# Moving row stores, weight casts, token pieces, two weight sums and one subtraction in a hand-ordered attention and two-MoE kernel

## The chip, the cores and the metric

The kernel runs as one program on one core of a Trainium2 chip. The metric is the device time of one execution in microseconds (us); before the change it is 2083.56 us, the median of three runs (2080.17 to 2083.95). A core has five engines with a queue each, worked off in order: TensorE (PE, with its weight loads as PEld), VectorE (DVE), ScalarE (ACT), GpSimd (POOL) and SyncE (SP, which here only issues DMAs). They meet at semaphores.

## The reference, cut to what matters

Linear attention with a positive feature map feeds a dense mixture of experts (all 8 experts for all tokens, weighted by a Sinkhorn-normalised gate), and its output feeds a second mixture in which each token goes to one expert.

```python
# attention: 4 x 8 heads, 576 tokens, head_dim 64, 128 features; x becomes 2304 tokens x 512
q_p, k_p = phi(q), phi(k)                  # phi: x @ w_phi minus its max |.|, exp(+) and exp(-)
attn = (q_p @ (k_p.T @ v)) / (q_p @ sum(k_p) + 1e-6)
# first MoE: E = 8 experts, D = 512, F = 1024
P = sinkhorn(exp(x @ w_gate - max))        # 8 rounds over rows and columns
x = sum(P[:, e] * (relu(x @ w1[e]) @ w2[e]) for e in range(8))
# second MoE: one expert for each token
logits = norm(x) @ norm(expert_emb).T / tau
idx, gate_w = argmax(logits, 1), softmax(logits).max(1)
out[mask_e] = gate_w * (relu(x[mask_e] @ w1[e]) @ w2[e])
```

## The kernel before

**Numbers.** Every fp32 operand of a large matmul is split into a high part (an fp32r copy, made by ACT) and a rest (source minus high part, made by DVE or POOL). A product is three matmuls for each pair: high by high, high by rest, rest by high.

**Stages.** Attention runs first (to about 222 us of the span). The first MoE then runs in 48 half-steps `h`: 16 groups `n` (an expert's half), each over three blocks of 768 tokens. Both layers of a group are written as Strassen-Winograd products: seven products of quarter matrices in place of eight. Groups 0, 1 and 15 ("plain", `p1_group` and `p2_plain`) use them for the first layer alone; groups 2 to 14 ("mixed", `layers`) for both layers, with 14 products of twelve matmuls in a half-step. The names are those of the algorithm: A11, S1, S2, ... are weight quarters and their sums, B11, T1, T2, ... token or hidden quarters and their differences; `hb["T1"]` is the hidden T1, `xs["T1"]` the tokens' T1. Then comes routing (logits, argmax, counting, an indirect scatter of token numbers into `ids`, and storing the token rows to `x2d` in DRAM), and the second MoE (`second`) runs over 22 blocks of 128 gathered rows, each with one expert's weights.

**Order.** Nothing is reordered by a scheduler: the instructions stand on each queue as the code emits them. A half-step is a generator that yields after each product; after each yield, the loop runs what a table (`sched`) holds for that half-step and tick (`run_at`). The numbers in the tables of `ops_at`, `route_steps` and `tail` are ticks: they set where an operation stands in the queues among the products. In `tail`, ticks from 40 on are in the last half-step, where ticks 40 to 53 follow its 14 first-layer products and 54 to 69 its 16 second-layer products.

**In `layers`** (lines 479 to 571) the hidden quarters are made on the way. After the product A22 the code adds `u2c` to its bank `b2`, makes T1's rest from bank `b0` (DVE), gates `b2` in place (DVE, line 442), copies B21's high part (ACT, line 471), and then subtracts `b0` from `r22` to get T2 (DVE, line 486) and copies T2's high part. The fourth product of the second layer, S1 by T1, goes to a new tile `Z = pair(qz)`, which takes the bank of `b0`; so it can begin only when every reader of `b0` is done.

**Weight preparation.** For mixed groups the weights of the next group are summed (`S1r`, `S3r`, `S2r`, `S4r`, POOL, line 351) and split (ACT line 345, POOL line 346) during the third half-step of a group, at ticks of `ops_at(h, ...)`. In the same half-step POOL also makes the rests of the hidden quarters (line 474).

**Token pieces.** In half-steps 0 and 1 the next block's token quarters are loaded ("load"), subtracted on DVE (T3a, T1a, T2a, T4a, line 390) and split (ACT line 382, DVE line 383), at ticks of the same kind.

**The end of the first MoE.** `route_steps(6, ...)` routes tokens 768 to 1535 in the last two half-steps: `route_s` and `route_w` (DVE) make the gate weight, and `route_w` then stores six pieces of 128 rows of 513 numbers with SP (line 954); the last two pieces lie in `raw` tiles. `load_regs` has SP read the block table, `load_raws` has SP load the first expert's eight weight pieces of 512 KB (line 1074). `start_second` opens a pool (`m2r`) over the region in which the token tiles and the `raw` tiles lay. `first_w1(0, (c,))` casts weight piece `c` into that pool (ACT line 1102), makes its rest (DVE line 1103), and has SP load the next block's piece if its expert differs. `load_ids` has SP read the scattered token numbers (line 1058), six small loads a block, and `gather` has POOL fetch the rows. SP's DMAs go round eight semaphores; a DMA waits until the one eight places ahead of it on SP's queue has landed.

Of the kernel before, what the change touches and what calls it, by code (L numbers as in the profile page):

```python
# [32 lines left out]
RB = 6  # L33
# [12 lines left out]
def build(tc, a, out):  # L46
# [14 lines left out]
    V, A, G, T, SP = nc.vector, nc.scalar, nc.gpsimd, nc.tensor, nc.sync  # L61
# [28 lines left out]
    ids = [dr.tile([NSLOT, 1], I32, name=f"ids{k}") for k in range(RB)]  # L90
# [347 lines left out]
    def gate(out, th, src):  # L438
        g_ = hb["gate"][:, th * TH:(th + 1) * TH]
        if len(src.shape) == 3:  # L440
            g_ = g_.unsqueeze(1).to_broadcast([P, 2, TH])
        V.scalar_tensor_tensor(out=out, in0=src, scalar=0.0, in1=g_, op0=ALU.max, op1=ALU.mult)
# [27 lines left out]
    def high(nm, src):  # L470
        A.copy(hb[nm][:, 0], src)  # L471

    def rest(nm, src, eng):
        eng.tensor_tensor(out=hb[nm][:, 1], in0=src, in1=f32(hb[nm][:, 0]), op=ALU.subtract)  # L474
# [6 lines left out]
    def layers(h, n, bi):  # L481
        odd = h % 2
        qx, qz = (0, 3) if odd else (3, 0)

        def tt(out, x, y, op=ALU.subtract):
            V.tensor_tensor(out=out, in0=x, in1=y, op=op)  # L486

        def read(q_, ps, op=ALU.add):
            z = acc(bi)[:, q_]
            V.tensor_tensor(out=z, in0=z, in1=ps, op=op)  # L490

        b0 = pair(qz)
        yield from twin(b0, 1, "A11", xs["B11"], True)
        m1c = hraw("a")
        A.copy(m1c, b0)  # L495
        yield
        for nm in ("B11", "T1", "B21", "B22"):
            hb[nm] = hp.tile([P, 2, 2, TH], F32R, tag="h" + nm, name=f"h{nm}")
        for nm in ("T2", "T3", "T4"):
            hb[nm] = live["h3"].tile([P, 2, 2, TH], F32R, tag="h" + nm, name=f"h{nm}")  # L500
        hx = dict(hb)
        hb["gate"] = gates.popleft()

        yield from twin(b0, 1, "S2", xs["T2"], False)
        u2c = hp.tile([P, 2, TH], F32, tag="tu", name="u2c")
        A.copy(u2c, b0)
        b1 = pair(1)
        yield from twin(b1, 1, "A12", xs["B21"], True)
        tt(b1, b1, m1c, ALU.add)
        r11 = hraw("b")  # L510
        gate(r11, 0, b1)
        high("B11", r11)
        yield from twin(b0, 1, "S1", xs["T1"], False)
        rest("B11", r11, G)
        vc = hraw("c")
        A.copy(vc, b0)
        b2 = pair(2)
        yield from twin(b2, 1, "S3", xs["T3"], True)
        tt(b1, b2, vc, ALU.add)
        r22 = hraw("d")  # L520
        gate(r22, 1, b1)
        high("B22", r22)
        for i, _ in enumerate(twin(b0, 1, "S4", xs["B22"], False)):
            if i == 0:
                rest("B22", r22, G)
            yield
        gate(b0, 1, b0)
        t3 = hraw("c")
        tt(t3, r22, b0)
        high("T3", t3)  # L530
        tt(b0, b0, r11)
        high("T1", b0)
        for i, _ in enumerate(twin(b2, 1, "A22", xs["T4"], False)):
            if i == 0:
                rest("T3", t3, G)
            yield
        tt(b2, b2, u2c, ALU.add)
        rest("T1", b0, V)
        gate(b2, 0, b2)
        high("B21", b2)  # L540
        tt(r22, r22, b0)
        high("T2", r22)
        X = pair(qx)
        for i, _ in enumerate(twin(X, 2, "A11", hx["B11"], True)):
            if i == 0:
                rest("T2", r22, G)
            yield
        Y = pair(1)
        yield from twin(Y, 2, "S4", hx["B22"], True)
        read(1, Y, ALU.subtract)  # L550
        read(0, X)
        rest("B21", b2, V)
        Z = pair(qz)
        yield from twin(Z, 2, "S1", hx["T1"], True)
        t4 = hraw("a")
        tt(t4, r22, b2)
        high("T4", t4)
        read(1, Z)
        for i, _ in enumerate(twin(Y, 2, "S3", hx["T3"], False)):
            if i == 0:  # L560
                rest("T4", t4, G)
            yield
        read(3, Y)
        yield from twin(X, 2, "S2", hx["T2"], False)
        read(1, X)
        W_ = pair(2)
        yield from twin(W_, 2, "A12", hx["B21"], True)
        read(0, W_)
        yield
        w22 = wt[2, "A22"]  # L570
        yield from twin(Z, 2, w22, hx["T4"], False)
        read(2, Z, ALU.subtract)
        yield
# [381 lines left out]

    def route_i(t0, i):
        si = rt[t0]["si"]
        G.indirect_dma_start(out=ids[i % RB], out_offset=bass.IndirectOffsetOnAxis(si[:, i:i + 1], 0), in_=tokid[:, t0 + i:t0 + i + 1], in_offset=None)

    meta = c0.tile([1, 3, NBLK], I32, name="meta")  # L960
    ebx = c0.tile([1, NBLK + 1], F32, name="ebx")
# [230 lines left out]
    def first_w1(i, cs):  # L1192
        for c in cs:
            wsplit(i, 1, c)
            wcond(i + 1, 1, c)
# [10 lines left out]
    def ops_at(h, table, ops):  # L1206
        for i, names in table:
            for nm in names.split():
                at_tick(h + i // 40, i % 40, ops[nm])
# [19 lines left out]
    for h, (n, bi) in enumerate(HS):  # L1229
        nxt = HS[h + 1][1] if h + 1 < NH else bi  # L1230
        if nxt != bi:
            if n:
                for nm in XMIX if mixed(n) else XUSE:
                    at_tick(h, XFREE[nm][mixed(n)], partial(xreload, nxt, XUSE.index(nm)))
            else:
                ops = x_tasks(nxt, scratch(h), V)
                if h == 0:
                    ops_at(h, ((filled[0], "load"), (18, "B11"), (19, "T3a T1a"), (20, "T2a T2"), (21, "T3"), (22, "T1"), (23, "B21 T4a"), (24, "T4"), (25, "B22")), ops)
                else:
                    ops_at(h, ((1, "load"), (3, "T3a"), (5, "T1a"), (7, "T2a"), (14, "T2"), (15, "T1"), (16, "B11"), (17, "T3"), (18, "B21"), (19, "T4a"), (20, "T4"), (21, "B22")), ops)  # L1240
        if h % NB == NB - 1 and n + 1 < NGR:
            o1, o2 = wops(1, n + 1), wops(2, n + 1, SL1 if n == 0 else SL15 if n == NGR - 2 else {})
            if mixed(n):
                ops_at(h, ((2, "A11"), (3, "S1r"), (4, "S3r"), (5, "S2r"), (8, "A12"), (9, "S4r"), (10, "S2"), (12, "S1"), (14, "S3"), (16, "S4"), (18, "A22 load")), o1)
            else:
                ops_at(h, ((8, "A11"), (9, "S1r"), (10, "S3r"), (11, "S2r"), (13, "A12"), (14, "S4r"), (16, "S2"), (18, "S1"), (20, "S3"), (22, "S4"), (24, "A22 load")), o1)
            if n == 0:
                ops_at(h, ((24, "A11"), (25, "A12"), (26, "A21"), (28, "A22 load")), o2)
            elif n == 1:
                ops_at(h, ((22, "S1r"), (23, "S3r"), (24, "A12"), (26, "A22"), (28, "S3"), (40, "A11"), (41, "S2r"), (42, "S4r"), (44, "S1"), (46, "S4"), (49, "S2 load")), o2)  # L1250
            elif n == NGR - 2:
                ops_at(h, ((18, "A11"), (24, "A21"), (28, "A12"), (40, "A22 load")), o2)
            else:
                ops_at(h, ((18, "A11"), (20, "S1r"), (21, "S3r"), (25, "S2r"), (40, "A12"), (41, "S4r"), (43, "S1"), (45, "A22"), (46, "S4"), (49, "S3"), (51, "S2 load")), o2)
        if h >= 2 * NB - 1 and h + 1 < NH:
            at_tick(h, 20, partial(load_gate, HS[h + 1][0] // 2, nxt))
        if n == NGR - 1:
            for k, (i, j, op) in enumerate(FROM_Z):
                at_tick(h, 2 + 2 * k, partial(z_op, bi, i, j, op, G))
# [25 lines left out]
    rf = first_blocks()  # L1285

    tail = route_steps(0, (2, 4, 6, 8, 10, 12), (1, 2, 3, 4, 5, 6), p=13, b=14, o=16, s=18, c=19, d=21, w=23, i=(23, 23, 24, 25, 26, 27))
    tail += route_steps(6, (26, 28, 40, 43, 45, 47), (25, 26, 27, 42, 43, 44), p=48, b=46, o=47, c=49, d=49, i=(50, 50, 50, 51, 53, 54), s=54, w=56)
    tail += [(k, partial(next, rf, None)) for k in (50, 51, 52, 53, 55)] + [(54, partial(load_regs, i)) for i in range(2)]
    tail += [(54, partial(load_raws, 1, range(4))), (54, partial(load_raws, 2, range(4))), (56, early_second), (56, start_second)]  # L1290
    tail += [(62 + 2 * c, partial(first_w1, 0, (c,))) for c in range(4)]
    tail += [(63 if i < 2 else 67, partial(load_ids, i)) for i in range(NEARLY)]
    tail += [(67, partial(gather, 0)), (68, partial(gather, 1))]
    for i in range(3):
# [53 lines left out]
    def second(i0, i1):  # L1348
# [15 lines left out]
        i = i0  # L1364
        if i0 == 0:
            t0 = NA
            for k in range(3, NTL - NA):
                route_l(t0, k)
                route_a(t0, k)
# [146 lines left out]
```

## Time and profile before

| | us |
|---|---|
| median of three runs | 2083.56 |
| the profiled execution | 2082.38 |
| its span | 2080.5 |
| TensorE busy in the span | 1978.9 (95%) |
| DVE, POOL, ACT busy | 1296.1 (62%), 1057.5 (51%), 868.2 (42%) |
| TensorE's granted clock, mean | 0.985 |

TensorE is the bound: it is busy 95% of the span, and the page's 40 slices show 9 tenths in nearly all of them. The exceptions are the first slice (8) and the seven slices from 32 on that read 9, 3, 8, 8, 9, 9, 9: slice 33 alone has 3 tenths, and there the clock row falls to 7 and 8. So the questions to such a profile are where TensorE sits idle, and who ends each wait. In the timeline a row is start, duration, engine, line, operation, out<-in, shapes, count, and in brackets the idle time before it and what ended it. In a table of stretches a row is the stretch, its length, then the busy time and the number of instructions of PE, PEld, DVE, ACT and POOL, the granted clock, the share of time of the DMA engines, and GB/s. In a table of waits a row is who waited for whom, the sum, the number of times, and the longest.

### The profile page before, as it was taken

To read this page: it belongs to the slowest core of one execution; us is meant where nothing else is said; L and a number is where in the kernel's file an instruction comes from. 1 tells how busy PE (TensorE), PEld (TensorE's weight loads), DVE (VectorE), ACT (ScalarE), POOL (GpSimd) and SP (SyncE) were. 2 spreads that over 40 slices of the span, in tenths; PEclk is the share of its full clock that TensorE was granted. 3 is DMA by queue.
4 is the path that set the end of the run, shared out by engine and by line. 5 is a ranking of instruction groups with operands and counts; after the bars stand their busy time and mean duration, and the time that the engine had idled before them with its cause. 6 is when DMAs were issued, how large, how long until landed. Compare 5 with 4: busy or idle time off the path is not lost. (4 is left out here: it accounts for less than half of the span.)

```text
span 2080.5 us, 31444 instructions
## 1 busy us (share of the span) xinstructions
PE 1978.9 (95%) x11627; PEld 1886.8 (91%) x11627; DVE 1296.1 (62%) x1838; ACT 868.2 (42%) x1391; POOL 1057.5 (51%) x811
## 2 busy tenths in 40 slices
PE   8999999999999999999999999999999993889998
PEld 8999989999999999999999999999999993778886
DVE  6766556466656655655665565565566452589996
ACT  5566432223332433333242333334233231668785
POOL 1256102566574846657484665748375431345543
PEclk9999999999999999999999999999999997899999
DMA  3345633553625435373543537263453366334861
GB/s 119 113 141 182 223 138 147 138 193 101 247 86 194 154 122 188 107 249 81 204 143 133 177 110 246 80 216 124 152 174 110 114 145 112 51 99 151 289 232 63
DMA packets 138287, 314.63 MB, mean 151 GB/s; under 512 B 30456, under 2 KB 85256, under 8 KB 138130
## 3 DMA queue, kind: packets, MB, share of 16 engines
q1 hardware_dynamic: 134034, 302.06, 44.8%
q0 software_dynamic: 4096, 10.51, 1.8%
q8 instruction: 94, 1.54, 0.3%
q14 instruction: 63, 0.52, 0.1%
HBM read 335.81 MB, written 32.28 MB: 177 GB/s over the span
## 5 line engine op out<-in xcount | busy, mean ns | idle before, releaser
L490 DVE TENSOR_TENSOR acca<-acca,Q 128x768 f32<-128x768 f32 x182 | 170.5, 952 | 157.8 <-PE Q L428 157.8
L346 POOL TENSOR_TENSOR w1A<-raw,w1A 128x512 fp32r<-128x512 f32 x48 | 62.0, 1291 | 212.7 <-ACT w1A L345 132.8
L426 PE MATMUL Q<-hT,w2S 128*128 128x384 f32 x468 | 159.5, 341 | 9.8 <-ACT hB L471 9.8
L474 POOL TENSOR_TENSOR hB<-rb,hB 128x768 fp32r<-128x768 f32 x39 | 71.9, 1844 | 179.7 <-PE Q L428 179.7
L426 PE MATMUL Q<-xT,w1S 128*128 128x384 f32 x468 | 156.4, 334 | 0.9 <-ACT ra L495 0.9
L427 PE MATMUL Q<-hT,w2S 128*128 128x384 f32 x468 | 156.6, 335 | 0.0
L428 PE MATMUL Q<-hT,w2S 128*128 128x384 f32 x468 | 156.5, 334 | 0.0
L428 PE MATMUL Q<-xT,w1S 128*128 128x384 f32 x468 | 156.4, 334 | 0.0
L427 PE MATMUL Q<-xT,w1S 128*128 128x384 f32 x468 | 156.3, 334 | 0.0
L490 DVE TENSOR_TENSOR accb<-accb,Q 128x768 f32<-128x768 f32 x91 | 85.0, 952 | 84.3 <-PE Q L428 84.3
L1103 DVE TENSOR_TENSOR s1l<-rw,s1h 128x1024 fp32r<-128x1024 f32 x88 | 106.2, 1251 | 47.1 <-ACT s1h L1102 47.1
L495 ACT COPY ra<-Q 128x768 f32<-128x768 f32 x39 | 31.3, 802 | 207.9 <-PE Q L428 172.8
L486 DVE TENSOR_TENSOR Q<-Q,ra 128x768 f32<-128x768 f32 x39 | 37.7, 966 | 124.6 <-PE Q L428 124.6
L1102 ACT CAST s1h<-rw 128x1024 fp32r<-128x1024 f32 x88 | 88.5, 1062 | 60.1 <-DMA x2d<-raw 37.5
L474 POOL TENSOR_TENSOR hT<-rd,hT 128x768 fp32r<-128x768 f32 x39 | 72.3, 1853 | 66.0 <-ACT hT L471 66.0
L426 PEld LDWEIGHTS Q<-hT,w2S 128*128 128x128 f32 x468 | 87.8, 188 | 19.8 <-ACT hB L471 19.8
L426 PE MATMUL Q<-xB,w1A 128*128 128x384 f32 x312 | 104.3, 334 | 0.7 <-DVE accb L843 0.7
L428 PE MATMUL Q<-xB,w1A 128*128 128x384 f32 x312 | 104.2, 334 | 0.0
L427 PE MATMUL Q<-xB,w1A 128*128 128x384 f32 x312 | 104.2, 334 | 0.0
L426 PE MATMUL Q<-hB,w2A 128*128 128x384 f32 x312 | 104.2, 334 | 0.0
L427 PE MATMUL Q<-hB,w2A 128*128 128x384 f32 x312 | 104.2, 334 | 0.0
L428 PE MATMUL Q<-hB,w2A 128*128 128x384 f32 x312 | 104.2, 334 | 0.0
(428 smaller groups left out, 6663.7 us busy)
## 6 DMA issues: line engine op xcount, KB each, us to landing
xT<-xpd SPq DMA_DIRECT2D x120, 768.0 KB
rw<-in_moe_w SPq DMA_DIRECT2D x176, 512.0 KB
xB<-xpd SPq DMA_DIRECT2D x90, 768.0 KB
raw<-in_moe_w SPq DMA_DIRECT2D x34, 512.0 KB
gate<-gd SPq DMA_DIRECT2D x45, 384.0 KB
rx<-in_moe_w SPq DMA_DIRECT2D x30, 512.0 KB
xpd<-xT SPq DMA_DIRECT2D x12, 768.0 KB
xpd<-xB SPq DMA_DIRECT2D x9, 768.0 KB
```

What stands on the lines that cost most here:

```text
L346: eng.tensor_tensor(out=t[:, 1], in0=r(nm), in1=f32(t[:, 0]), op=ALU.subtract)
L426: T.matmul(bank, w[:, 0, j, k, :], x[:, 0, k, :], start=start and k == 0, stop=False, skip_group_check=True)
L427: T.matmul(bank, w[:, 0, j, k, :], x[:, 1, k, :], start=False, stop=False, skip_group_check=True)
L428: T.matmul(bank, w[:, 1, j, k, :], x[:, 0, k, :], start=False, stop=stop and k == 1, skip_group_check=True)
L474: eng.tensor_tensor(out=hb[nm][:, 1], in0=src, in1=f32(hb[nm][:, 0]), op=ALU.subtract)
L486: V.tensor_tensor(out=out, in0=x, in1=y, op=op)
L490: V.tensor_tensor(out=z, in0=z, in1=ps, op=op)
L495: A.copy(m1c, b0)
L1102: A.copy(hi, r)
L1103: V.tensor_tensor(out=lo, in0=r, in1=f32(hi), op=ALU.subtract)
```

## The change

It moves things and neither adds nor removes an instruction on the computing engines (`ids[i % RB]` becomes `ids[i]`, which is the same tile for the values of `i` that occur).

- In `layers`, the subtraction for T2 and the copy of its high part stand ahead of B21's gate and copy.
- In mixed groups, the sums `S1r` and `S3r` for the next group's first layer are made at ticks 4 and 8 of the second half-step, not at ticks 3 and 4 of the third.
- In half-steps 0 and 1 the token pieces stand at other ticks, one at a time and two ticks apart towards the end; in half-step 1 the first subtractions move from ticks 3, 5 and 7 to 14 and 15.
- At the end of the first MoE, `route_s` moves from tick 54 to 50 and `route_w` with its stores from 56 to 52; the steps of the block table (`rf`) and the weight loads move one tick later. The casts of the first block's weights move from ticks 62, 64, 66, 68 to 65, 67, 69 and, for the fourth, into `second`. The loads of token numbers for blocks 0 and 1 stay at tick 63.

```diff
@@ layers
         rest("T1", b0, V)
+        tt(r22, r22, b0)
+        high("T2", r22)
         gate(b2, 0, b2)
         high("B21", b2)
-        tt(r22, r22, b0)
-        high("T2", r22)
@@ token pieces, half-step 1
-                    ops_at(h, ((1, "load"), (3, "T3a"), (5, "T1a"), (7, "T2a"), (14, "T2"), (15, "T1"), (16, "B11"), (17, "T3"), (18, "B21"), (19, "T4a"), (20, "T4"), (21, "B22")), ops)
+                    ops_at(h, ((2, "load"), (14, "T3a T1a"), (15, "T2a B11"), (16, "T2"), (18, "T3"), (20, "T1"), (22, "B21 T4a"), (24, "T4"), (26, "B22")), ops)
@@ weight sums of mixed groups
-                ops_at(h, ((2, "A11"), (3, "S1r"), (4, "S3r"), (5, "S2r"), (8, "A12"), ...
+                ops_at(h - 1, ((4, "S1r"), (8, "S3r")), o1)
+                ops_at(h, ((2, "A11"), (5, "S2r"), (8, "A12"), ...
@@ routing and the first weights
-    tail += route_steps(6, ..., p=48, b=46, o=47, c=49, d=49, i=(50, 50, 50, 51, 53, 54), s=54, w=56)
-    tail += [(k, partial(next, rf, None)) for k in (50, 51, 52, 53, 55)] + [(54, partial(load_regs, i)) for i in range(2)]
-    tail += [(54, partial(load_raws, 1, range(4))), (54, partial(load_raws, 2, range(4))), (56, early_second), (56, start_second)]
-    tail += [(62 + 2 * c, partial(first_w1, 0, (c,))) for c in range(4)]
+    tail += route_steps(6, ..., p=47, b=46, o=47, c=49, d=49, i=(50, 50, 50, 51, 53, 54), s=50, w=52)
+    tail += [(k, partial(next, rf, None)) for k in (51, 52, 53, 54, 56)] + [(55, partial(load_regs, i)) for i in range(2)]
+    tail += [(55, partial(load_raws, 1, range(4))), (55, partial(load_raws, 2, range(4))), (56, early_second), (56, start_second)]
+    tail += [(65 + 2 * c, partial(first_w1, 0, (c,))) for c in range(3)]
@@ second, i0 == 0
             t0 = NA
+            first_w1(0, (3,))
```

DVE in a mixed half-step, as a difference (`Q_341` is the bank `b2`, `Q_339` the bank `b0`, `rd` is `r22`):

```order
 L486 TENSOR_TENSOR Q_341_5110<-Q_341_5110,u2c 128x2x384
 L474 TENSOR_TENSOR hT_5038<-Q_339_5012,hT_5038 128x768
+L486 TENSOR_TENSOR rd<-rd,Q_339_5012 128x768
 L442 SCALAR_TENSOR_TENSOR Q_341_5110<-Q_341_5110,gate_2_4919 128x2x384
-L486 TENSOR_TENSOR rd<-rd,Q_339_5012 128x768
 L490 TENSOR_TENSOR accb<-accb,Q_343_5185 128x768
```

The last DVE instruction that reads `b0` now stands one place sooner, and the gate of `b2` one place later; the rest of DVE's order is as it was.

SP at the end of the first MoE, before (`rows6a` to `raw` are the six pieces of token rows, `rw` the weight pieces):

```order
L1074 ISA
L1074 DMA rw_3_15982<-in_moe_w 128x1024
L954 DMA x2d<-rows6a 128x513
L954 DMA x2d<-rows6b 128x513
L954 DMA x2d<-rows6c 128x513
L954 DMA x2d<-rows6d 128x513
L954 DMA x2d<-raw_15602 128x513
L954 DMA x2d<-raw_15603 128x513
L1074 ISA
L1074 DMA rw_0_15968<-in_moe_w 128x1024
```

and in the changed kernel, at the place where the stores now stand:

```order
L954 DMA x2d<-rows_2_15264 128x2x513
L954 DMA x2d<-rows6a 128x513
L954 DMA x2d<-rows6b 128x513
L954 DMA x2d<-rows6c 128x513
L954 DMA x2d<-rows6d 128x513
L954 DMA x2d<-raw_15602 128x513
L954 DMA x2d<-raw_15603 128x513
L1045 TENSOR_LOAD meta
```

The six stores were behind all eight weight loads; now they follow the first batch's stores, ahead of the reads of the block table, and the eight weight loads and the twelve loads of token numbers come behind them.

POOL around a group's third half-step, before (`hT` and `hB` are rests of hidden quarters, `ws` and `raw` weight sums):

```order
L474 TENSOR_TENSOR hT_6063<-ra,hT_6063 128x768
L346 TENSOR_TENSOR w1A_4_6288<-raw_5684,w1A_4_6288 128x512
L351 TENSOR_TENSOR ws_4_6297<-raw_5686,raw_5684 128x512
L351 TENSOR_TENSOR raw_5686<-raw_5684,raw_5686 128x512
L351 TENSOR_TENSOR raw_5684<-ws_4_6297,raw_5684 128x512
L346 TENSOR_TENSOR w1A_4_6346<-raw_5686,w1A_4_6346 128x512
```

and in the changed kernel:

```order
L351 TENSOR_TENSOR ws_4_6070<-raw_5686,raw_5684 128x512
L351 TENSOR_TENSOR raw_5686<-raw_5684,raw_5686 128x512
L474 TENSOR_TENSOR hB_6057<-rb,hB_6057 128x768
L474 TENSOR_TENSOR hB_6060<-rd,hB_6060 128x768
L474 TENSOR_TENSOR hT_6062<-rc,hT_6062 128x768
L474 TENSOR_TENSOR hT_6061<-rd,hT_6061 128x768
L474 TENSOR_TENSOR hT_6063<-ra,hT_6063 128x768
L346 TENSOR_TENSOR w1A_4_6291<-raw_5684,w1A_4_6291 128x512
L351 TENSOR_TENSOR raw_5684<-ws_4_6070,raw_5684 128x512
L346 TENSOR_TENSOR w1A_4_6346<-raw_5686,w1A_4_6346 128x512
```

Two of the three sums went from between the first two weight splits to ahead of the second half-step's five rests.

## Rows read from the trace of the kernel before

**Rows 1.** Busy time by stretch: the gap, and the second MoE after 1831 us.

```profile
1735.00:1765.00 30.00, 0.77 (x7) 0.68 (x7) 1.60 (x2) 2.64 (x5) 0.00 (x0) 0.58 0.79 185
1831.00:2080.50 249.50, 241.67 (x1159) 199.61 (x1159) 218.69 (x230) 183.40 (x240) 120.36 (x108) 0.99 0.51 172
```

**Rows 2.** Waits of TensorE over the whole span, the three longest in total.

```profile
PE psD L426 <- DVE accb L843: 30.8, 2, 29.4
PE Q L427 <- POOL hT L474: 17.1, 13, 1.4
PE Q L426 <- ACT hB L471: 9.8, 26, 0.4
```

**Rows 3.** Timeline of SP's queue, 1720 to 1766 us: weight loads, then row stores.

```profile
1726.58 5.60 SPq L1074 DMA_DIRECT2D rw<-in_moe_w  x8
1738.20 0.34 SPq L954 DMA_DIRECT2D x2d<-rows6a  x1
...
1743.30 1.60 SPq L954 DMA_DIRECT2D x2d<-raw  x2
```

**Rows 4.** Timeline of ACT and PE, 1762 to 1785 us: the gap's end.

```profile
1762.32 1.99 ACT L1102 CAST s1h<-rw 128x1024 fp32r<-128x1024 f32 x2 [37.54 <-DMA x2d<-raw]
...
1765.15 0.69 PE L426 MATMUL psD<-hT,w2A 128*128 128x384 f32 x1 [29.38 <-DVE accb L843]
...
1784.17 0.59 PE L1131 MATMUL psA<-s1h,xth 128*128 128x512 f32 x1 [0.17 <-ACT xth L1114]
```

**Rows 5.** Busy time by stretch of 5 us; the last two numbers are DMA share, GB/s.

```profile
1686.00:1691.00 5.00, 5.00 (x37) 5.00 (x37) 1.69 (x7) 0.00 (x0) 3.87 (x4) 1.00 1.38 102
1691.00:1696.00 5.00, 5.00 (x36) 4.96 (x36) 0.59 (x2) 2.32 (x6) 3.76 (x3) 1.00 0.43 4
...
1701.00:1706.00 5.00, 5.00 (x40) 4.96 (x39) 1.95 (x4) 2.15 (x5) 2.03 (x3) 1.00 1.05 83
...
1725.00:1730.00 5.00, 4.97 (x28) 4.97 (x29) 2.60 (x14) 0.00 (x0) 0.97 (x2) 1.00 0.87 13
...
1755.00:1760.00 5.00, 0.00 (x0) 0.00 (x0) 0.00 (x0) 0.00 (x0) 0.00 (x0) 0.50 0.59 57
```

**Rows 6.** First batch: its stores on SP's timeline; its scatters' DMAs, median us to landing.

```profile
1687.35 1.82 SPq L954 DMA_DIRECT2D x2d<-rows  x3
...
ids<-tokid,si POOLq DMA_INDIRECT x6, 22.8
```

**Rows 7.** Timeline of DVE, 1720 to 1723 us: a hidden rest, then the block table's end.

```profile
1720.29 0.56 DVE L449 TENSOR_TENSOR hB<-psA,hB 128x384 fp32r<-128x384 f32 x1 [0.54 <-ACT hB L448]
...
1722.83 0.15 DVE L1016 SCALAR_TENSOR_TENSOR meta<-ei,fl 1x6 int32<-1x6 f32 x1
```

**Rows 8.** Timeline of PE and DVE in one mixed half-step, 626 to 632 us.

```profile
626.65 0.33 PE L426 MATMUL Q<-hB,w2A 128*128 128x384 f32 x1
...
628.73 0.33 PE L426 MATMUL Q<-hB,w2S 128*128 128x384 f32 x1
...
629.40 0.96 DVE L442 SCALAR_TENSOR_TENSOR Q<-Q,gate 128x768 f32<-128x768 f32 x1
...
630.26 0.94 DVE L486 TENSOR_TENSOR rd<-rd,Q 128x768 f32<-128x768 f32 x1
...
631.36 0.41 PE L426 MATMUL Q<-hT,w2S 128*128 128x384 f32 x1 [0.38 <-ACT hB L471]
```

**Rows 9.** Timeline of POOL and PE in a group's third half-step, 589 to 612 us.

```profile
589.97 1.29 POOL L346 TENSOR_TENSOR w1A<-raw,w1A 128x512 fp32r<-128x512 f32 x1 [3.00 <-ACT w1A L345]
...
611.80 0.44 PE L427 MATMUL Q<-hT,w2A 128*128 128x384 f32 x1 [1.35 <-POOL hT L474]
```

**Rows 10.** Timeline of PE and DVE in half-steps 0 and 1.

```profile
250.89 0.44 PE L426 MATMUL psD<-hT,w2A 128*128 128x384 f32 x1 [1.22 <-ACT accb L841]
...
263.14 0.96 DVE L390 TENSOR_TENSOR xq<-xq,xq 128x768 f32<-128x768 f32 x1 [4.02 <-DMA xq<-xd]
...
264.62 0.44 PE L426 MATMUL psA<-xT,w1S 128*128 128x384 f32 x1 [3.05 <-DVE hB L436]
```

More of the change, by code (lines that the diff above doesn't have):

```diff
@@ L957, in route_i @@
         si = rt[t0]["si"]
-        G.indirect_dma_start(out=ids[i % RB], out_offset=bass.IndirectOffsetOnAxis(si[:, i:i + 1], 0), in_=tokid[:, t0 + i:t0 + i + 1], in_offset=None)
+        G.indirect_dma_start(out=ids[i], out_offset=bass.IndirectOffsetOnAxis(si[:, i:i + 1], 0), in_=tokid[:, t0 + i:t0 + i + 1], in_offset=None)
     meta = c0.tile([1, 3, NBLK], I32, name="meta")
@@ L1237, in build @@
                 if h == 0:
-                    ops_at(h, ((filled[0], "load"), (18, "B11"), (19, "T3a T1a"), (20, "T2a T2"), (21, "T3"), (22, "T1"), (23, "B21 T4a"), (24, "T4"), (25, "B22")), ops)
+                    ops_at(h, ((filled[0], "load"), (17, "B11"), (18, "T3a T1a"), (19, "T2a"), (20, "T2"), (22, "T3"), (24, "T1"), (26, "B21 T4a"), (28, "T4"), (29, "B22")), ops)
                 else:
-                    ops_at(h, ((1, "load"), (3, "T3a"), (5, "T1a"), (7, "T2a"), (14, "T2"), (15, "T1"), (16, "B11"), (17, "T3"), (18, "B21"), (19, "T4a"), (20, "T4"), (21, "B22")), ops)
+                    ops_at(h, ((2, "load"), (14, "T3a T1a"), (15, "T2a B11"), (16, "T2"), (18, "T3"), (20, "T1"), (22, "B21 T4a"), (24, "T4"), (26, "B22")), ops)
         if h % NB == NB - 1 and n + 1 < NGR:
@@ L1243, in build @@
             if mixed(n):
-                ops_at(h, ((2, "A11"), (3, "S1r"), (4, "S3r"), (5, "S2r"), (8, "A12"), (9, "S4r"), (10, "S2"), (12, "S1"), (14, "S3"), (16, "S4"), (18, "A22 load")), o1)
+                ops_at(h - 1, ((4, "S1r"), (8, "S3r")), o1)
+                ops_at(h, ((2, "A11"), (5, "S2r"), (8, "A12"), (9, "S4r"), (10, "S2"), (12, "S1"), (14, "S3"), (16, "S4"), (18, "A22 load")), o1)
             else:
@@ L1287, in build @@
     tail = route_steps(0, (2, 4, 6, 8, 10, 12), (1, 2, 3, 4, 5, 6), p=13, b=14, o=16, s=18, c=19, d=21, w=23, i=(23, 23, 24, 25, 26, 27))
-    tail += route_steps(6, (26, 28, 40, 43, 45, 47), (25, 26, 27, 42, 43, 44), p=48, b=46, o=47, c=49, d=49, i=(50, 50, 50, 51, 53, 54), s=54, w=56)
-    tail += [(k, partial(next, rf, None)) for k in (50, 51, 52, 53, 55)] + [(54, partial(load_regs, i)) for i in range(2)]
-    tail += [(54, partial(load_raws, 1, range(4))), (54, partial(load_raws, 2, range(4))), (56, early_second), (56, start_second)]
-    tail += [(62 + 2 * c, partial(first_w1, 0, (c,))) for c in range(4)]
+    tail += route_steps(6, (26, 28, 40, 43, 45, 47), (25, 26, 27, 42, 43, 44), p=47, b=46, o=47, c=49, d=49, i=(50, 50, 50, 51, 53, 54), s=50, w=52)
+    tail += [(k, partial(next, rf, None)) for k in (51, 52, 53, 54, 56)] + [(55, partial(load_regs, i)) for i in range(2)]
+    tail += [(55, partial(load_raws, 1, range(4))), (55, partial(load_raws, 2, range(4))), (56, early_second), (56, start_second)]
+    tail += [(65 + 2 * c, partial(first_w1, 0, (c,))) for c in range(3)]
     tail += [(63 if i < 2 else 67, partial(load_ids, i)) for i in range(NEARLY)]
```

## The prediction, as it was made before the changed kernel ran

> **What bounds the kernel now.** I read the slices of the page first: TensorE (PE) is full nearly everywhere, and one slice stands out. Then the table of PE's waits over the whole span [rows 2]: there, who holds PE up is a short list. Two long waits for DVE's `accb` hold 30.8 us, 29.4 of them in one gap; 13 waits for a hidden rest of POOL hold 17.1; 26 waits that are put down to ACT's B21 copy hold 9.8. The stretch of the gap shows that PE works 0.77 of 30 us and that everything else stands too, while the DMAs move 185 GB/s [rows 1]: the gap belongs to DMAs. Behind it the second MoE keeps PE busy 241.67 of 249.5 us [rows 1], so a shift of its start lasts to the end. Last come the timelines of each wait. PE is the bound, so an edit is worth what it takes out of PE's idle time, and everything else counts only where it makes PE wait.
>
> **T2's difference ahead of B21's gate (mixed half-steps).** Products start 2.08 us apart (626.65, 628.73 [rows 8]); the fourth, S1, starts 2.63 after the third, at 631.36, with 0.38 idle. Its bank was `b0`, and DVE's `r22 -= b0` is the last reader: it starts at 630.26, takes 0.94, ends at 631.20, and PE starts 0.16 behind it. The row names ACT's B21 copy, but by the code B21's copy touches `b2`, not the bank that S1 writes. With the change the subtraction takes the gate's place at 629.40 and ends near 630.34; with the 0.16 the bank is free at 630.5, while S4 keeps PE until 628.73 + 2.08 = 630.81. The wait goes, with 0.31 to spare. Gain for each: 2.63 - 2.08 = 0.55, and the 0.41 of the first matmul behind it falls to the usual 0.33, 0.08 more; I take 0.62. There are 39 mixed half-steps, but in 13 of them POOL's wait (below) follows within the half-step and would swallow the gain, so 26 x 0.62 = **-16.1**. The smaller end is the idle time alone, 9.8; the larger, with a third of the other 13, some 19. Cost: the gate of B21 ends 0.9 later and its copy too. B21 enters a product only after S1 and later ones, several products of 2.08 on, and DVE's order is otherwise the same; I put it at nothing. If that cover were gone, it would be 0.9 a time, which is a rival.
>
> **Two weight sums a half-step sooner.** They leave POOL's queue in the third half-step, where POOL's rest of T4 ends 1.35 late for PE at 611.80 [rows 9], 13 times. That would be 17.1 us [rows 2]. But the run of POOL's work that ends late starts at 589.97, after POOL stood idle for 3.00 us, and what it waited for is ACT's copy of a weight quarter [rows 9]. That copy stands on ACT where it stood. The two sums were made ahead of that idle time, so taking them away makes the idle time longer and moves nothing behind it. I take **0**; bounds 0 and -17.1. In the second half-step the sums go ahead of five hidden rests; POOL is idle there for many microseconds, as its 51% share suggests, so no loss beyond two sums of at most 1.3 each [rows 9], of which PE sees nothing.
>
> **Token pieces in half-steps 0 and 1.** Two waits of PE stand there: 1.22 behind ACT (an `accb` copy that queued behind a piece's cast) and 3.05 behind DVE's hidden rest, because DVE was blocked for 4.02 us at 263.14 in a piece's subtraction that waited for its load [rows 10]. In half-step 1 the first subtraction goes from tick 3 to 14, some twenty microseconds later, and the load is long in. Both waits go: -4.27, and some 0.1 for the slower first matmul (0.44 against 0.33 [rows 8, 10]) each: **-4.4**. The pieces now stand late, up to tick 26; a late one could make half-step 2 wait, for at most what one piece costs, 1 to 2 us. Bounds -5.5 and -2.
>
> **The end of the first MoE.** Now: eight weight loads are issued at 1726.58, the six row stores behind them at 1738.20 to 1744.9, since each of SP's DMAs waits until the one eight ahead has landed [rows 3]. ACT's first cast waits 37.54 us for the last `raw` store, since its pool lies over the `raw` tiles, and starts at 1762.32; PE, which stopped at 1765.15 - 29.38 = 1735.8, goes on at 1765.15, and the second MoE's first product is at 1784.17 [rows 4].
>
> After: the stores follow the first batch's and only wait for `route_w` on DVE. That has four ticks less ahead of it: the hidden rest ends at 1720.85, and eight small operations of 0.15 stand behind it [rows 7], so the stores are issued from about 1722.1. The weight loads come behind the block table, near 1729. How long do the six stores take? Bounds from rows of the same bytes (1.58 MB): at the 102 GB/s in which the first batch began [rows 5] 15.4 us, or 17 with issue; and the first batch itself, issued at 1687.35 [rows 6], fell to 4 GB/s at 1691 to 1696 and still moved 83 GB/s at 1701 to 1706 [rows 5], so over 19 us; the scatters that ran beside it landed 22.8 us after issue [rows 6]. The new place is like the first batch's: scatters of POOL are on their way there too. I take 24 us: landed at 1746. (Fast 1739; slow 27 us, 1749; and if the weight loads behind them start as slowly as those at 1726.58, which moved 13 GB/s at 1725 to 1730 [rows 5], 1755.) The last stores before ended no better: 57 GB/s at 1755 to 1760 [rows 5]. The first cast moves from 1762.32 to 1746, -16.3. From there to the first product it was 21.85 us [rows 4]; some of this shortens, because the loads of the token numbers now stand ahead of the next weights on SP and PE has done three more ticks before it stops (near 1737.7): 0 to 4, I take 2. Together **-18.3**, bounds -27 and -8. PE's gap falls from 29.4 to about 11 us.
>
> The clock: in the gap the granted clock averages 0.58 [rows 1], which is full speed first and then half (1.2 of 2.4 GHz), and the first matmul behind it takes 0.69 [rows 4] against 0.33 [rows 8]. PE had stood for 29 us; about 11 still stay. I keep the slow restart as it is. The Trainium skill ("TensorE: Matmul & The Clock Gate", section "What's actually happening") says that the throttled state is the default and that activity releases it; by that a shorter gap that still idles would restart at half speed too, as taken here. Only if the engine came back at full speed would some 4 us more go: about 2040.
>
> The Trainium skill ("DMA: Bandwidth & Descriptors", section "Queues, rings and completion order") also says that each DMA engine takes the descriptors of a ring in order, which speaks against part of the gain: the first weight piece, 512 KB, would start only behind the stores, and at the gap's mean of 185 GB/s [rows 1] an estimate of its time is 2.8 us; the sum would be 2047 instead of 2044. That lies inside the bounds above.
>
> **The sum.** -16.1 - 0 - 4.4 - 18.3 = -38.8. The profiled execution took 2082.38 (1.2 below the median of 2083.56): **2043.6**.
>
> **Rivals.** (1) Slow drain: the stores and the weights behind them crawl as in the first batch, the first cast is at 1755, the tail gives 8 only: 2054. For it, the 4 and 13 GB/s [rows 5]; against it, only part of the scatters is still to be issued at 1722. (2) Fast drain, tail -27 (or a gap so short that the clock stays up): 2035. For it, the 102 GB/s; against it, both batches of stores before. (3) The two sums do free POOL: 17.1 us more, 2026. Against it stands the 3.00 us idle of POOL. (4) The moved difference buys nothing, since S1 is then held by something that was hidden behind it (T1's high copy on ACT, or a bank of PE's): mixed half-steps gain 0 to 4, 2056 to 2060. Against it, 0.31 to spare. (5) The other side: the row [rows 2, 8] is right in naming ACT's B21 copy, S1 (or DVE's queue behind the gate) depends on it, and the copy now comes 0.86 later (630.26 - 629.40). Then each of 39 half-steps loses 0.86, 33.5 us, in place of the 16.1: 2082.4 - 22.7 + 33.5 = 2093. It decides against the whole change once S1 starts more than 0.58 us later than now (22.7 / 39). Against it: the code, and that PE starts 0.16 behind DVE's end.
>
> **How the numbers follow.** Forecast 0.60; (1) 0.17; (2) 0.07; (3) 0.05; (4) 0.07; (5) 0.04. The range from 2031 to 2059 leaves out (3), (5) and the far ends of (2) and (4), together under 2 in 10. All cases but (5) are faster by much more than 0.2% (about 4 us, what a measurement of this kernel can tell from no change); within 0.2% needs (5) at part of its price together with a slow drain: 0.03. Faster 0.93, same 0.03, slower 0.04.
>
> **What would show it.** The profile after should have S4 to S1 at 2.08 in the mixed half-steps and no waits for ACT's B21 copy; POOL's 13 waits of 1.35 still there; no waits near 250.9 and 264.6; the stores some 16 us sooner than now, beyond the shift from the half-steps ahead; one gap of PE of about 11 us, then the half clock; and 249.5 us from there on as before. I would be wrong if POOL's waits go, if the stores take over 30 us, or if S1 waits longer than 0.4.

## The result

The changed kernel takes 2052.37 us (median of four runs, 2048.70 to 2055.02) against 2083.19 us of the kernel before: the ratio is 0.9853, 95% interval 0.9833 to 0.9874, so 26 to 35 us less. The forecast was 2043.6, the range 2031 to 2059. The profiled execution has a span of 2046.8 us, 33.7 less than before; it is the fastest of the four. Run once more beside other kernels, the changed kernel came to 0.9848 (0.9825 to 0.9871), which leaves out one run of 2425.88 us at a granted clock of 0.747.

Where these 33.7 us lie can be read from PE's timeline: four waits that both kernels have (near attention's end, L152 for ACT's `kvz`; the gate's matmul at L789; the first product of the mixed half-steps, L426 for `accb`; and the first wait behind them, L426 for `acca`) cut the span into stretches. All numbers are microseconds.

| stretch | before | after | difference | forecast |
|---|---|---|---|---|
| attention, up to the wait at L152 | 202.96 | 202.34 | -0.6 | 0 |
| from there to the gate's matmul, with half-steps 0 and 1 | 138.67 | 131.81 | -6.9 | -4.4 |
| from there to the mixed half-steps | 85.66 | 85.69 | 0.0 | 0 |
| mixed half-steps | 1192.10 | 1175.25 | -16.9 | -16.1 |
| the rest, to the end | 461.11 | 451.71 | -9.4 | -18.3 |

So the total came as near as it did partly by luck: two errors of opposite sign met. The last stretch gave half of what was forecast, and the token pieces gave more.

The waits of PE after, longest first (who waited for whom, the sum, how many times, the longest), answer to [rows 2]:

```profile
PE Q L427 <- POOL hT L474: 18.7, 13, 1.5
PE psB L877 <- ACT rows L879: 17.4, 4, 15.7
PE psD L1146 <- ACT hr L1141: 8.1, 1, 8.1
PE psA L1132 <- DVE gt L1117: 5.0, 3, 4.6
PE Q L427 <- POOL hB L474: 2.4, 13, 0.2
```

The 26 waits that were put down to ACT's B21 copy are gone. POOL's 13 are still there and are a little longer, 18.7 in place of 17.1. The gap of 29.4 has become one of 15.7, and the wait for `hr` behind it, 4.7 before, is 8.1.

PE and DVE in a mixed half-step after, for [rows 8]; in a timeline the columns are start, duration, engine, line and operation:

```profile
616.59 0.33 PE L426 MATMUL Q<-hB,w2A 128*128 128x384 f32 x1
...
618.66 0.33 PE L426 MATMUL Q<-hB,w2S 128*128 128x384 f32 x1
...
620.75 0.33 PE L426 MATMUL Q<-hT,w2S 128*128 128x384 f32 x1
```

```profile
619.34 0.94 DVE L486 TENSOR_TENSOR rd<-rd,Q 128x768 f32<-128x768 f32 x1
620.20 0.96 DVE L442 SCALAR_TENSOR_TENSOR Q<-Q,gate 128x768 f32<-128x768 f32 x1
```

S1 starts 2.09 after S4 and not 2.63; DVE's difference ends at 620.28, 0.47 before S1. The gate of B21 is now the later one of the two, as the order said, and nobody on PE waits for it.

The end of the first MoE after, SP's queue, for [rows 3] (`x8` is a run of eight issues, the duration spans the run, and `idr` are the token numbers):

```profile
1696.10 0.33 SPq L954 DMA_DIRECT2D x2d<-rows6a  x1
...
1697.98 1.47 SPq L954 DMA_DIRECT2D x2d<-raw  x2
1704.22 20.80 SPq L1074 DMA_DIRECT2D rw<-in_moe_w  x8
1725.74 12.23 SPq L1058 DMA_DIRECT2D idr<-ids  x12
1738.32 0.53 SPq L1074 DMA_DIRECT2D rw<-in_moe_w  x2
1740.78 17.44 SPq L1058 DMA_DIRECT2D idr<-ids  x24
1758.60 10.74 SPq L1074 DMA_DIRECT2D rw<-in_moe_w  x10
```

The same queue before, behind the stores:

```profile
1765.01 7.11 SPq L1058 DMA_DIRECT2D idr<-ids  x12
...
1774.95 17.42 SPq L1058 DMA_DIRECT2D idr<-ids  x24
1792.75 4.84 SPq L1074 DMA_DIRECT2D rw<-in_moe_w  x7
```

ACT and PE in the same stretch, for [rows 4]:

```profile
1725.71 1.04 ACT L1102 CAST s1h<-rw 128x1024 fp32r<-128x1024 f32 x1 [27.21 <-DMA rw<-in_moe_w]
...
1758.69 1.99 ACT L1102 CAST s1h<-rw 128x1024 fp32r<-128x1024 f32 x2 [10.07 <-DMA rw<-in_moe_w]
```

```profile
1728.01 1.11 PE L877 MATMUL psB<-ident,accb 128*128 128x128 f32 x4 [15.69 <-ACT rows L879]
...
1745.76 0.78 PE L1131 MATMUL psA<-s1h,xth 128*128 128x512 f32 x1
...
1763.12 1.11 PE L1146 MATMUL psD<-ident,hr 128*128 128x128 f32 x4 [8.09 <-ACT hr L1141]
```

and the two places behind the first product before:

```profile
1792.91 1.04 ACT L1102 CAST s1h<-rw 128x1024 fp32r<-128x1024 f32 x1 [5.45 <-DMA rw<-in_moe_w]
...
1796.40 1.12 PE L1146 MATMUL psD<-ident,hr 128*128 128x128 f32 x4 [4.67 <-ACT hr L1141]
```

To compare with before, add 24.3 us (1619.39 - 1595.09, what was won ahead of here). The stores go out at 1720.4 on the clock of before, 17.8 us sooner than in [rows 3]. The first cast stands at 1750.0 there, 12.3 sooner, and the first product of the second MoE at 1770.1, 14.1 sooner. But at 1763.12 the kernel is at 1787.4, and the same matmul stood at 1796.40 before: of the 14.1 only 9.0 are left. The second MoE from there on runs as in [rows 1], by the stretches of the profile after (the stretch, its length, then busy time of PE, PEld, DVE, ACT, POOL, the granted clock, DMA share, GB/s):

```profile
1797.00:2046.80 249.80, 241.86 (x1159) 199.73 (x1159) 220.51 (x228) 184.13 (x241) 119.07 (x104) 0.99 0.51 171
```

And the row stores themselves, for [rows 5]: 66 and 83 GB/s over 21 us, which is their 1.58 MB, then the weights behind them.

```profile
1696.00:1706.00 10.00, 9.38 (x46) 9.07 (x45) 6.32 (x26) 0.51 (x1) 3.72 (x4) 0.84 0.98 66
1706.00:1717.00 11.00, 6.32 (x44) 5.96 (x42) 1.12 (x2) 0.00 (x0) 0.00 (x0) 0.97 0.99 83
1717.00:1726.00 9.00, 0.00 (x0) 0.00 (x0) 0.00 (x0) 0.29 (x1) 0.00 (x0) 0.50 1.00 172
```

### The profile page after: what moved, and what is told of

Read it like the earlier page. It is cut to its first block, busy times and chain, and to the rows that moved or that the text cites. A ratio compares the mean times of both kernels' runs of the same rounds, so it can differ in the third digit from the quotient of the medians.

```text
span 2046.8 us, 31493 instructions
## 1 busy us (share of the span) xinstructions
PE 1969.2 (96%) x11627; PEld 1888.7 (92%) x11627; DVE 1295.8 (63%) x1838; ACT 869.2 (42%) x1391; POOL 1055.7 (52%) x811
## 4 chain that ended last, share of the span: by engine, by line
PE 62%; POOL 11%; DVE 9%; issue 8%; DMA 6%; SPq 2%; ACT 2%; POOLq 0%; DVEq 0%; ACTq 0%
PE Q L427 14%; PE Q L426 14%; PE Q L428 14%; DMA rw<-in_moe_w 4%; POOL w1S L346 3%; PE psD L206 3%; DVE s2l L1103 2%; PE psD L426 2%; PE psD L427 2%; POOL hT L474 2%; PE psD L428 2%; PE psA L426 2%; PE psA L428 2%; PE psA L427 2%; POOL w1A L346 2%
## 5 line engine op out<-in xcount | busy, mean ns | idle before, releaser
L426 PE MATMUL Q<-xT,w1S 128*128 128x384 f32 x468 | 156.4, 334 | 0.9 <-ACT ra L495 0.9
L426 PE MATMUL Q<-hT,w2S 128*128 128x384 f32 x468 | 156.3, 334 | 0.0
L426 PE MATMUL Q<-xB,w1A 128*128 128x384 f32 x312 | 104.3, 334 | 0.7 <-DVE accb L843 0.7
L474 POOL TENSOR_TENSOR hT<-ra,hT 128x768 fp32r<-128x768 f32 x39 | 71.4, 1830 | 64.3 <-ACT hT L471 64.3
L426 PE MATMUL Q<-hB,w2A 128*128 128x384 f32 x312 | 104.2, 334 | 0.0
L1103 DVE TENSOR_TENSOR s2l<-rw,s2h 128x1024 fp32r<-128x1024 f32 x76 | 92.7, 1262 | 9.4 <-ACT s2h L1102 4.9
```

The source lines that it names most:

```text
L426: T.matmul(bank, w[:, 0, j, k, :], x[:, 0, k, :], start=start and k == 0, stop=False, skip_group_check=True)
L1103: V.tensor_tensor(out=lo, in0=r, in1=f32(hi), op=ALU.subtract)
```

## The experiments

**The four parts, each alone in the kernel before.** First T2's difference.

```diff
+        tt(r22, r22, b0)
+        high("T2", r22)
         gate(b2, 0, b2)
         high("B21", b2)
-        tt(r22, r22, b0)
-        high("T2", r22)
```

> The kernel before with one edit: T2's difference and copy ahead of B21's gate and copy. My theory: S1 is held by DVE's difference, not by ACT's copy of B21, so the spacing from S4 to S1 falls from 2.62 to 2.08 in 26 of the 39 mixed half-steps and stays near 2.6 in the 13 third ones, where POOL's rest of a hidden quarter holds the product ahead of it; about -16.1 to -17 us, near 2066. Rival: the row is right that ACT's copy of B21 holds S1: then this kernel is slower than before, by 20 to 34 us.

Ratio 0.9912 (0.9896 to 0.9929), 2063.49 us. The mixed half-steps take 1175.46 us in its trace; in the other three kernels with one part alone, which lack this edit, 1191.9 to 1192.2. So the edit is worth 16.5 to 16.7 us, S1 waited for DVE, and the rival is out. In the 13 third half-steps S1 still starts 2.57 after S4 (2.62 before): POOL's rest `hB` holds the second matmul of S4 there (the 13 waits of 0.2 in the list above). POOL's longer waits belong to this edit too:

```profile
PE Q L427 <- POOL hT L474: 18.8, 13, 1.5
```

The end of the first MoE alone (ticks of `route_s`, `route_w`, the block table, the weight loads and the casts, as in the diff of the change):

> The kernel before with only the edits at the end of the first MoE (routing ticks, stores ahead of the weight loads, weight casts later). From the trace of the changed kernel the stretch behind the mixed half-steps is 9.4 us shorter, so 2073 to 2074. If the slow part in the changed kernel came from the other edits (the shift of everything by 24 us), the gain here would be nearer to the forecast 18.3: 2064.

Ratio 0.9960 (0.9948 to 0.9973), 2073.54 us: 5.6 to 10.8 less, near the 9.4 and not near the 18.3. PE's longest gap is 13.18 us here, with a wait of 8.6 for `hr` behind it. The shortfall is the part's own.

The token pieces alone:

> The kernel before with only the new ticks of the token pieces in half-steps 0 and 1. Theory: two waits of 4.3 us go and with the 3.05 one the half clock behind it (granted clock 0.72 over 264 to 270 us, 1.7 us lost), together -6.9: 2076. Rival: the waits alone, -4.4: 2079.

Ratio 0.9957 (0.9944 to 0.9970), 2072.17 us, so 6.2 to 11.7 less. The stretch of half-steps 0 and 1 took 131.8 to 133.4 us in the nine traces with the new ticks, and 138.7 to 142.5 in the five with the old ones. Part of the spread with the old ticks is the clock. These are the stretches behind the wait of 3 us, before, after, and in the kernel with only the new end of the first MoE (old ticks):

```profile
264.00:270.00 6.00, 5.21 (x19) 4.23 (x20) 4.83 (x9) 1.35 (x3) 0.00 (x0) 0.72 0.07 23
```

```profile
264.00:270.00 6.00, 6.00 (x37) 4.85 (x37) 4.81 (x9) 2.40 (x6) 0.00 (x0) 1.00 0.01 3
```

```profile
267.00:270.00 3.00, 2.53 (x10) 2.21 (x11) 2.44 (x5) 0.49 (x1) 0.00 (x0) 0.76 0.02 5
270.00:274.00 4.00, 3.83 (x13) 3.33 (x12) 2.96 (x6) 0.86 (x2) 0.00 (x0) 0.50 0.01 4
```

In six microseconds the old ticks ran 19 matmuls and the new ones 37. Behind a wait of 3 us the granted clock stood at its lower level (1.2 of 2.4 GHz) for some 3 to 7 us: 0.72 over 6 us is 3.4 us of it; 0.76 over 3, 0.50 over 4 and 0.89 over the 6 behind these are 6.8. In the profile before that cost (1 - 0.72) x 6 = 1.7 us, in another execution more. A forecast that counts the waits alone prices such a change too low.

The two sums alone:

> The kernel before with only the two weight sums made one half-step sooner. Theory: 0 (within 2 us), POOL's 13 waits stay at 1.35 since the run of work that ends late begins with a wait for ACT's copy. Rival: the waits shrink, up to -17.1.

Ratio 0.9998 (0.9986 to 1.0009), 2080.55 us. Its waits of PE for POOL:

```profile
PE Q L427 <- POOL hT L474: 17.1, 13, 1.4
```

They are those of [rows 2]: the sums do nothing for PE. The 3.00 us for which POOL stood idle in [rows 9] have grown, as the prediction took it, and the work behind them is as late as before:

```profile
590.92 1.29 POOL L346 TENSOR_TENSOR w1A<-raw,w1A 128x512 fp32r<-128x512 f32 x1 [5.61 <-ACT w1A L345]
```

**What holds the end of the first MoE: SP's queue.** First the changed kernel again, as the measure on the same chip.

> The changed kernel once more, beside its variants: 0.985 of the kernel before, about 2051.

0.9848 (0.9825 to 0.9871); the three runs behind it took 2047.95, 2049.83 and 2053.50 us. Beside it the first variant:

```diff
-    tail += [(63 if i < 2 else 67, partial(load_ids, i)) for i in range(NEARLY)]
+    tail += [(63 if i < 2 else 67, partial(load_ids, i)) for i in range(3)]
...
             first_w1(0, (3,))
+            load_ids(3)
...
             w2_this(0, no, (0, 1))
+            load_ids(4)
...
             w2_this(0, no, (2, 3))
+            load_ids(5)
```

> The changed kernel; the loads of token numbers for blocks 3, 4 and 5 are issued later on SP, behind the loads of the second block's weight pieces 2 and 3 (and 4 and 5 behind more of them). Theory: in the changed kernel SP's queue of such loads has become the limit: ACT's cast at 1758.69 waits 10.07 us for a weight load that stands on SP behind 24 small loads of 0.5 us, and PE waits 8.09 us behind it at 1763.12. With the change that wait falls by 3 to 8 us: 0.2 to 0.4% faster than the changed kernel, 2043 to 2048, and the stretch from the first product of the second MoE to PE's return is shorter by as much. Rival: ACT or DVE are late there anyway (the casts themselves): no change.

0.9823 (0.9806 to 0.9840), 2046.14 us. The wait of 8.1 us for `hr` is gone from the list of PE's waits, and the queue of SP reads

```profile
1740.37 3.02 SPq L1058 DMA_DIRECT2D idr<-ids  x6
1743.76 0.52 SPq L1074 DMA_DIRECT2D rw<-in_moe_w  x2
1746.17 2.84 SPq L1058 DMA_DIRECT2D idr<-ids  x6
1749.37 4.94 SPq L1074 DMA_DIRECT2D rw<-in_moe_w  x6
```

where the two weight loads come 3.4 us behind the start of the small loads ahead of them and not 17.8 us. The stretch behind the mixed half-steps takes 446.3 us against 452.3 in the changed kernel beside it: 6.0 us. The theory holds; the intervals of the two ratios overlap, and the trace decides. These weight loads are skipped (the second block has the first one's expert), so ACT waited 10 us for SP to reach an instruction that moves nothing. The kernel before had this wait too, 5.45 us.

**What holds it: the row stores.** The rows of `x2d` lie 640 numbers (2560 bytes) apart, not 513 (2052 bytes); the numbers between them are zeroed once at the start.

```diff
-    x2d = dr.tile([NT + 1, XW], F32, name="x2d")
+    x2d = dr.tile([NT + 1, 640], F32, name="x2d")
...
-            SP.dma_start(out=x2d[o:o + m * P, :].rearrange("(t p) d -> p t d", p=P), in_=rows)
+            SP.dma_start(out=x2d[o:o + m * P, 0:XW].rearrange("(t p) d -> p t d", p=P), in_=rows)
```

> The changed kernel; the rows of x2d in DRAM lie 640 numbers apart, not 513, so that each stored row of 2052 bytes begins at a multiple of 512 bytes (the rest of each row is zeroed once, early). Theory: the six stores drain slowly (28 us for 1.58 MB, packets of 0.4 us) since their rows cross lines of the DRAM at odd places; aligned, they drain in 4 to 10 us, PE's gap of 15.7 us falls below 6 and the time by 4 to 10 us. Rival: the drain is slow for another reason (many small packets, the scatters beside them): same drain, same time as the changed kernel.

0.9805 (0.9789 to 0.9822), 2042.86 us. SP issues the stores at 1699.43 and all eight weight loads within 7.04 us, where they took 20.80, since the stores ahead of them land sooner; PE's gap is 5.43 us, not 15.7 (lines stand one further down in this kernel):

```profile
1708.73 7.04 SPq L1075 DMA_DIRECT2D rw<-in_moe_w  x8
```

```profile
1721.08 1.12 PE L878 MATMUL psB<-ident,accb 128*128 128x128 f32 x4 [5.43 <-ACT rows L880]
```

The same in the kernel before, with nothing else changed but the zeros:

> The kernel before with nothing changed but the distance of x2d's rows, 640 numbers and not 513 (zeroed once, early). Theory: the stores there drain in 12 to 14 us behind the weight loads because of the rows' odd places; aligned, they land near 1750 and not at 1762, PE's gap of 29.4 falls to 16 to 20, and the kernel is 8 to 13 us faster: 2070 to 2075. Rival: what counts there is that the stores stand behind 4 MB of weights; then the gain is below 3 us.

0.9981 (0.9969 to 0.9993), 2074.87 us. The two stretches in which the six stores drained, in the kernel before and here, behind the weights in both and with no other work beside them:

```profile
1747.00:1759.00 12.00, 0.00 (x0) 0.00 (x0) 0.00 (x0) 0.00 (x0) 0.00 (x0) 0.50 0.97 102
```

```profile
1749.00:1755.00 6.00, 0.00 (x0) 0.00 (x0) 0.00 (x0) 0.59 (x1) 0.00 (x0) 0.50 0.70 250
```

The same six stores went at 250 GB/s in place of 102, by the distance of the rows alone. With it each row begins at a multiple of 512 bytes and no longer borders on the next; which of the two counts was not tried. PE's gap fell to 18.44 us, as expected. The time fell by 1.5 to 6.4 us, less than the 8 to 13 expected. In the traces the stretch behind the mixed half-steps is 11.0 us shorter (450.1 against 461.1), and attention is 2.8 longer, the price of the zeros (below). The Trainium skill ("DMA: Bandwidth & Descriptors", section "Specifications") asks for transfers of at least 512 bytes for full rate. Rows of 2052 bytes fulfil that and yet ran at 102 GB/s, so here the measurement decides. The same section of the Trainium skill gives a read and a write back as what smaller transfers cost; whether the ends of rows at odd places pay that too, no run here shows.

Both edits in the changed kernel:

> Both of these edits in the changed kernel. If both theories hold, the gains add: 8 to 18 us below the changed kernel, 2033 to 2043. If only SP's queue was the limit, as the variant with later loads of token numbers.

0.9765 (0.9747 to 0.9783), 2035.50 us: the gains add. The stretch behind the mixed half-steps takes 434.9 us, 17.4 less than in the changed kernel, where the two edits alone took out 6.0 and 10.1. The same kernel on another occasion:

> The changed kernel with later loads of token numbers and with rows 640 numbers apart, once more beside the next two: 2035.

0.9817 (0.9799 to 0.9836), 2040.45 us. The two intervals for one kernel do not meet, so between occasions a ratio moves by more than its interval says, here by 0.5%; the two traces have spans of 2035.9 and 2033.9. Differences of that size are read from the traces' stretches, or from kernels that ran beside each other.

**What slows the first microseconds of the stores: the scatters.** Even with the wider rows the stores began slowly. In the kernel beside `best_again` the second batch's six scatters of token numbers (POOL) go behind the stores:

```diff
-... i=(50, 50, 50, 51, 53, 54), s=50, w=52)
+... i=(58, 58, 58, 59, 59, 59), s=50, w=52)
```

> As the kernel beside it (both edits), with the second batch's six scatters moved from ticks 50 to 54 to ticks 58 and 59, behind the row stores. In all traces so far packets of the row stores take 1.5 to 4 us each for some 4 to 6 us while POOL issues scatters. Theory: the scatters hold the store packets up, so here the stores drain without that stretch, in 6 to 8 us and not 13, and the slow stretch moves to where the scatters now stand, into the weight loads; the time changes little (within 4 us either way). Rival: the slow stretch belongs to the start of the stores, whatever POOL does: it stays where it is.

0.9820 (0.9796 to 0.9844), 2043.03 us, the same as the kernel beside it. Its stretches, first the stores, then the weights behind them, in two parts:

```profile
1701.00:1707.00 6.00, 5.45 (x22) 5.14 (x22) 5.21 (x25) 0.51 (x1) 2.78 (x3) 0.73 0.72 263
1709.00:1716.00 7.00, 7.00 (x49) 6.96 (x48) 1.67 (x3) 0.00 (x0) 2.68 (x3) 1.00 1.00 39
1716.00:1728.00 12.00, 7.35 (x33) 6.93 (x33) 2.37 (x3) 4.73 (x9) 0.00 (x0) 0.72 0.99 136
```

In the same place with the scatters ahead (the kernel with wider rows alone):

```profile
1701.00:1706.00 5.00, 4.38 (x21) 4.04 (x20) 3.64 (x14) 0.51 (x1) 2.94 (x3) 0.82 1.33 57
1706.00:1712.00 6.00, 6.00 (x40) 6.00 (x38) 1.67 (x3) 0.00 (x0) 0.00 (x0) 1.00 0.75 224
```

Without scatters ahead of them the stores move all their bytes in 6 us at 263 GB/s. The slow stretch has gone to the weight loads, which now follow the scatters, with 39 GB/s. So the slowness goes with the scatters and not with the stores; what it costs is only moved. Why the weights then stay at 136 GB/s is not shown. The DMA share of about 1 beside 39 GB/s shows that the queues hold packets and do not idle. The slow starts in [rows 5], of stores (4 GB/s) and of weights (13 GB/s), both behind scatters, fit this; there it was not tried.

**The zeros.** The unused numbers of each wider row had been zeroed at the start; here one copy in the middle of the first MoE fills them.

```diff
-        SP.dma_start(out=x2d[0:NT, XW:640]..., in_=zrow[:, 0:127]...)
+    at_tick(4, 3, lambda: SP.dma_start(out=x2d[0:NT, XW:640], in_=a["moe2_w1"]...[0:NT, 0:640 - XW]))
```

> As the changed kernel with both edits (later loads of token numbers, rows 640 numbers apart), but the 127 unused numbers of each row are filled by one copy from DRAM in the middle of the first MoE, not by zeros at the start. In the runs with zeros PE waited 3.8 to 5.7 us near 18 to 20 us of the span, where the changed kernel waits 0.7. Theory: these zeros' packets delayed the first loads of attention; without them 3 to 5 us less: 2030 to 2036. Rival: the wait comes and goes by itself, the same time as with zeros, 2036 to 2040.

0.9751 (0.9732 to 0.9771), 2035.34 us, where the kernel before ran at 2086.82. Attention ends at 203.31 in its trace, and at 204.9 to 207.5 in the traces with zeros; the wait of 3.8 to 5.7 us at 18 to 20 us is gone, with one of 0.74 at 16 us as in the changed kernel (0.67). That much is shown; the ratio alone could not tell it. This version has the lowest ratio of all that ran, 1% below the changed kernel, though its interval overlaps that of the kernel with both edits and zeros (0.9747 to 0.9783).

## Why the prediction was right or wrong

**T2 ahead of B21's gate: right, step by step.** Forecast -16.1, measured -16.5 to -16.9. The row named ACT's copy, the code named DVE; the difference now ends before S4 does. The 13 third half-steps gave nothing, as taken, but the reason was incomplete: the wait inside S4 for POOL's `hB` already absorbs it, ahead of the wait for T4.

**The two sums: right.** 0, with POOL's idle time as the reason, which grew from 3.00 to 5.61; rival (3) is out.

**The token pieces: the mechanism was right, the size was not.** The step "Both waits go: -4.27, and some 0.1 for the slower first matmul" left out the clock behind a wait of 3 us: 4.4 was forecast, 6.9 came in these two traces, and 7 to 11 over the executions with old ticks. The clock is 1.7 of the missing 2.5 us; the rest was not followed. The trace of before showed it: the stretch from 264 us had a granted clock of 0.72, and that stretch was not read.

**The end of the first MoE: right in sign, twice too large.** Three terms are at fault.
- "I take 24 us" for the stores: they were issued at 1696.10, and the semaphore of the last one was complete at 1724.6, 28.5 us later. (Their packets had ended at 1717.9. From there to the last completion it was 6.7 us, with the weight loads moving behind them, and 2.4 in the kernel before, where nothing moved behind them; why is open.) The first batch had been the right row; its slow drain is the one of rival (1), and both things found above to slow such stores, the distance of the rows and scatters on their way, were present here as there. The stores did go out 1.7 us sooner than forecast.
- "would start only behind the stores", of the first weight piece: this rule of the Trainium skill ("DMA: Bandwidth & Descriptors", section "Queues, rings and completion order") was put aside as within the bounds. The trace agrees with it: up to 1717 us the DMAs moved 66 x 10 + 83 x 11 = 1.57 MB, the six stores, though the first weight load was issued at 1704.22; and ACT's first cast ends its wait on the weight load [27.21 <-DMA rw], one microsecond behind the last store. It cost 1.1, not the 2.8 that it was estimated at.
- "From there to the first product ... I take 2", and then 249.5 us as before: the first held (1.8), the second did not. The step that failed is that whatever is won at the first product is kept to the end. Behind it stood SP's queue, before as after: 36 small loads, with two weight loads among them, then the loads for which ACT's next casts wait. SP came to the first small load 15.0 us sooner (1725.74 + 24.3 against 1765.01). But the first twelve took 12.23 us and not 7.11: eight places ahead of them now stand the weight loads, still on their way, where before stood the stores for the most part, which had landed. The 24 behind them began only 9.9 us sooner (1740.78 + 24.3 against 1774.95), and that is about what the end of the kernel kept. That the loads of the token numbers stand ahead of the next weights was counted as a gain; it is what took 5 us of it back.

**The clock** at the gap came out as taken: PE stood for 15.7 us, the granted clock averages 0.65 from 1711 to 1729, and the first matmul of a product behind the gap takes 0.67 us in place of 0.33:

```profile
1711.00:1729.00 18.00, 2.31 (x14) 1.99 (x13) 1.23 (x1) 2.22 (x4) 0.00 (x0) 0.65 0.99 181
```

```profile
1730.48 0.67 PE L426 MATMUL psD<-hB,w2A 128*128 128x384 f32 x1
```

## What to carry to other kernels

When a gap closes, follow the queue of the engine that only issues: what is won at the first product is kept only if the skipped and small DMAs in front of the next needed load also move. Price a wait with the clock behind it, not by its own length. And when a store is slow for its bytes, look at where its rows begin and at what other DMAs run beside it before moving it about: here the wider rows alone took 10.1 us out of the last stretch of the changed kernel (452.3 to 442.2), as much as the whole reordering of the stores and casts had won there (9.4).

## What the runs showed of the hardware

- Row stores of 2052 bytes to DRAM drained at 102 GB/s with rows 2052 bytes apart and at 250 to 263 GB/s with rows 2560 bytes apart, where no scatter stood ahead of them.
- Six scatters of 128 single numbers each, issued by POOL, held up whatever large transfer came behind them: 39 GB/s over 7 us for weight loads that moved 417 GB/s at 1740 to 1745 us of the kernel before. Why six transfers of 512 bytes do that is open.
- Behind a wait of 3 us on PE the granted clock stood at its lower level for 3 to 7 us, in executions of the same stretch by unlike amounts; without the wait it stayed at 1.00.
